# Mixing the weights of the last 1024 tokens one step apart instead of two, in a fused attention and feed-forward kernel

## The chip, the cores and the metric

The kernel runs on one core of one Trainium2 chip. The metric is the device time of one execution in microseconds (us). TensorE is called PE below, VectorE DVE, ScalarE ACT, GpSimd POOL and SyncE SP.

## The reference, cut to what matters

```python
# attention: B, H, S, D = 4, 8, 768, 64; n_global = 8, n_local = 96
scores = scale * q @ k.T + bias            # only a band of 96 keys and 8 global keys is kept
a = softmax(scores)
x = (a @ v)                                # reshaped to 3072 tokens x 512
# feed-forward part, d_model 512, d_ff 1024
a = x @ w1
b = x @ w2
h = a * b @ w3
return h @ w_out
```

The tolerance wants nearly float32 accuracy, so each float32 operand is held as a rounded high part and a low part, and each product is made of three matmuls (high by high, high by low, low by high).

## The kernel before, in words

The tokens come in 12 chunks of 256 (four batches of three). Attention runs in 24 steps of two head pairs, two steps for a chunk. The first four steps (0 to 3) are woven by hand with the loading of the weights. The steps 4 to 23 are the loop at lines 924 to 945, and the change is in this loop.

A step does the following. `visit` puts on PE the score matmuls of step s (L528) and, between them, the products of the probabilities with the values of step s - 2 (L637). `rows` makes the biased scores on DVE (L544) and the exponentials on ACT (L545), eight of each. `take` copies the finished attention output out of PSUM (L58 on ACT, L59 on DVE). `back` brings the transposed probabilities of the step before back from memory. `softmax` scales the rows, half of them on ACT (L561) and half on DVE (L563), after two small DVE instructions (L549, L550). `send` transposes on DVE (L598) and writes the result to memory (L600, on SP's queue); in a step in which a batch begins it also clears part of the tile on POOL (L592).

In between, `slices(k)` lets the feed-forward part of earlier chunks (`FeedForward.run`) go on by k pieces. Most pieces are six matmuls of 128x512 on PE. A product in PSUM tile m (L222 to L224) is emptied by ACT (L230) or multiplied by DVE (L232) and then split in high and low (L58, L59); one in PSUM tile o (L255 to L257) is emptied by ACT (L261). There are two PSUM buffers for m and o together, so the product after the next one needs its buffer emptied.

The last 1024 tokens are not done by `run` but after the loop, by a Strassen scheme (`strassen`), which needs sums and differences of blocks of w1 and w2. These are what `mix`, `round_off` and `keep` make, for one of eight weight groups f at a time:

- `mix(f)` on POOL: two additions that put high and low together (L902, into the tile tq) and four subtractions of blocks (L905, into the tile tl).
- `round_off` : ACT rounds tl to th (L910), and POOL takes th from tl in two instructions (L912), which leaves the low part in tl.
- `keep` on SP's queue: two DMAs of 512 KB write th and tl to the tensor tw in memory (L916, L917).

`strassen` reads tw with the loads of L985. The tiles tq, th and tl have one buffer each, so L905 of the next group waits until L917 has read tl.

The orders on PE, ACT, POOL and SP in the loop are those of the program (`manual_schedule`). An engine's instruction that waits holds everything behind it on that engine. The order on DVE is made by the framework's scheduler.

In the kernel before, the mix of group f is put out at the end of step 7 + 2f, and its rounding and writing in step 8 + 2f, so that the last group is written in step 22.

```python
    SLICES = [()] * 3 + [14, 7, 7, 6, 6, 6] + [10, 10] + [9] * 7 + [8, 8, 7, 7, 7, 9]
```

Of the kernel before, what the change touches and what calls it, by code (L numbers as in the profile page):

```python
# [27 lines left out]
NFC = DF // P  # L28
# [5 lines left out]
SLOT = GLB + P  # L34
KW = WIN + NQ * SLOT
BW = WIN + GLB
MIX = 7
UW = BW + P
QW = KW + T
STEP = 2  # L40
# [399 lines left out]
def banded(ctx, tc, ff, xp, ns, nt, one, nf, oki, ident, qk, vx):  # L440
# [68 lines left out]
    def load_values(c, hp, tag="vr"):  # L509
        b, cb = divmod(c, NCB)  # L510
        nw = 2 * NQ if cb else 2 * NQ - 1
        vr = ld.tile([P, STEP, 2 * NQ, 2 * D], F32, tag=tag, name=f"vr_{c}_{hp}")
        nc.sync.dma_start(out=vr[:, :, :nw], in_=vx[b, cb, hp // STEP, :, :, :nw])
        return [vr[:, i] for i in range(STEP)]
# [16 lines left out]
    def rows(c, hp, ps, sm=None):  # L531

        pr = at.tile([P, NQ, 2, UW], F32, tag="pr", name=f"pr_{c}_{hp}")
        mx = at.tile([P, NQ, 2], F32, tag="mx", bufs=3, name=f"mx_{c}_{hp}")
        if sm is None:
            sm = at.tile([P, NQ, 2], F32, tag="sm", bufs=3, name=f"sm_{c}_{hp}")
        for j in range(NQ):
            first = c % NCB == 0 and j == 0
            w0 = BW if first else 0
            for u in range(2):  # L540
                h = 2 * hp + u
                bias = bias0[:, h, :] if first else biasw[:, h, :]
                m = mx[:, j, u:u + 1]
                nc.vector.tensor_tensor_reduce(out=pr[:, j, u, w0:], in0=ps[u][:, j, w0:UW], in1=bias, scale=-SCALE, scalar=3.0e38, op0=ALU.add, op1=ALU.min, accum_out=m)  # L544
                nc.scalar.activation(pr[:, j, u, w0:], pr[:, j, u, w0:], AF.Exp, bias=m, scale=-1.0, accum_out=sm[:, j, u:u + 1])  # L545
        return pr, sm
# [5 lines left out]
    def softmax(c, hp, pr, sm, scaled, inverted=False):  # L552

        if not inverted:
            invert(sm)
        for j in range(NQ):
            w0 = BW if c % NCB == 0 and j == 0 else 0
            for u in range(2):
                x, r = pr[:, j, u, w0:], sm[:, j, u:u + 1]
                if u == 0 or scaled is nc.scalar:  # L560
                    nc.scalar.activation(x, x, AF.Copy, scale=r)  # L561
                else:
                    nc.vector.tensor_scalar(out=x, in0=x, scalar1=r, scalar2=None, op0=ALU.mult)  # L563
        return pr
# [37 lines left out]
    def back(s):  # L602
        if s not in sent:
            return
        x, d = sent.pop(s)
        for b, m0 in enumerate((1, 0, 3, 2)):
            ms = slice(m0, m0 + 5)
            (nc.sync, nc.scalar)[b // 2].dma_start(out=x[b * BK:(b + 1) * BK].rearrange("r k a u c -> r (k a) (u c)")[:, ms], in_=d[:, :, :, b].rearrange("k a r e -> r (k a) e")[:, ms])
        phs[s] = x
# [37 lines left out]
    def slices(k):  # L647
        while k > 0 and work:
            if next(work[0], "end") == "end":
                work.pop(0)  # L650
            else:
                k -= 1

    def loads(s, keys=True, vals=True):
        if s < n and keys:
            qrs[s] = load(*pairs(s)[0])
        if s < n and vals:
            vrs[s] = load_values(*pairs(s)[0])
# [10 lines left out]
    def take(s, uu, late=False):  # L669
        c, h0 = pairs(s)[0]  # L670
        x2 = xs[c // 2]
        if c >= TAIL:
            x = x2[:, h0:h0 + STEP, c % 2 * T:][:, :, :T]
            for o, y in [(x, uu[:, :, :T])] if not isinstance(uu, list) else [(x[:, i], y[:, :T]) for i, y in enumerate(uu)]:
                nc.scalar.activation(o, y, AF.Copy)
            return
        xc = [x[:, :, c % 2 * T:][:, :, :T] for x in x2]
        hi, lo = (x[:, h0:h0 + STEP] for x in xc)
        if late:
            nc.scalar.activation(hi, uu[:, :, :T], AF.Copy)  # L680
            ff.late.append((lo, uu[:, :, :T], hi))
        else:
            for x in [(hi, lo, uu[:, :, :T])] if not isinstance(uu, list) else [(hi[:, i], lo[:, i], x[:, :T]) for i, x in enumerate(uu)]:
                split(nc, *x)
        if h0 + STEP == NP and c < 2:
            work.append(ff.run(c, *xc, c * T, T))
        elif h0 + STEP == NP and c % 2:
            work.append(ff.run(c, *x2, (c - 1) * T, W))

    def visit(s, sv, ahead):  # L690


        uu = None if sv is None else spread(sv)
        ps = [None, None]

        def some(i):
            ps[i] = scores(*pairs(s)[i], qrs[s][i])

        def half(k):
            if uu is not None:  # L700
                if k:
                    nc.scalar.activation(uu[:, :, T], ident[:, :STEP], AF.Copy)
                values([uu[:, i] for i in range(STEP)], sv, k)

        if ahead:
            some(0)
        half(0)
        if not ahead:
            some(0)
        some(1)  # L710
        half(1)
        return ps, uu
# [31 lines left out]
    def send(s, prs):  # L744
        for i, (pr, sm) in enumerate(prs):
            swap(s, i, pr)
# [150 lines left out]
    def mix(f):  # L897

        th, tl = tg.tile([P, 4, 2 * P], F32R, name="th"), tg.tile([P, 4, 2 * P], F32, name="tl")
        q = tg.tile([P, 2, NCC * P], F32, name="tq")  # L900
        for i in range(2):
            nc.gpsimd.tensor_tensor(out=q[:, i], in0=ff.wq[0][:, f, i].bitcast(F32), in1=ff.wq[1][:, f, i].bitcast(F32), op=ALU.add)  # L902
        (b11, b21), (b12, b22) = ((q[:, i, :2 * P], q[:, i, 2 * P:]) for i in range(2))
        for o, x, y in ((2, b12, b11), (0, b22, tl[:, 2]), (1, b22, b12), (3, b21, tl[:, 0])):
            nc.gpsimd.tensor_tensor(out=tl[:, o], in0=x, in1=y, op=ALU.subtract)  # L905
        mixed.append((f, th, tl))

    def round_off():
        f, th, tl = mixed[-1]
        nc.scalar.activation(th, tl, AF.Copy)  # L910
        for i in range(0, 4, 2):
            nc.gpsimd.tensor_tensor(out=tl[:, i:i + 2], in0=tl[:, i:i + 2], in1=th[:, i:i + 2].bitcast(F32), op=ALU.subtract)  # L912

    def keep():
        f, th, tl = mixed.pop(0)
        nc.sync.dma_start(out=tw[f, :, 0], in_=th.bitcast(F32))  # L916
        nc.sync.dma_start(out=tw[f, :, 1], in_=tl)  # L917

    SLICES = [()] * 3 + [14, 7, 7, 6, 6, 6] + [10, 10] + [9] * 7 + [8, 8, 7, 7, 7, 9]
    with tc.manual_schedule(engines={mybir.EngineType.PE}):  # L920
        with tc.manual_schedule(engines={mybir.EngineType.DVE, mybir.EngineType.SP}):
            first_steps()
        with tc.manual_schedule(engines={mybir.EngineType.Activation, mybir.EngineType.SP, mybir.EngineType.Pool}):
            for s in range(SWAP + 1, n):
                sv = s - 2 if s > SWAP + 1 else None
                ps, uu = visit(s, sv, True)
                rs = []
                for i, p in enumerate(pairs(s)):
                    rs.append(rows(*p, ps[i]))
                    if i == 0 and uu is not None:  # L930
                        take(sv, uu)
                loads(s + 1, vals=False)
                loads(s - 1, keys=False)
                back(s - 1)
                if 0 <= s - MIX < 2 * NFC and (s - MIX) % 2:
                    round_off()
                slices(2)
                for p, r in zip(pairs(s), rs):
                    softmax(*p, *r, nc.vector)
                send(s, rs)  # L940
                if mixed:
                    keep()
                if 0 <= s - MIX < 2 * NFC and (s - MIX) % 2 == 0:
                    mix((s - MIX) // 2)
                slices(SLICES[s] - 2)
            back(n - 1)
            vrs[n - 1] = load_values(*pairs(n - 1)[0], tag="qr")
            x0 = xs[TAIL // 2]
            ah = {k: both(xp, t, k) for k, t in (("a11", "xh"), ("a12", "xl"))}
            for i, y in enumerate(ah.values()):  # L950
                slices(3)
                split(nc, y[:, 0], y[:, 1], x0[:, i * NCC // 2:][:, :NCC // 2])
            slices(SLICES[n - 1] - 6)
            last_visit()
        ctx.close()
        strassen(tc, ff, xp, tw, x0, xs[TAIL // 2 + 1], ah, slices)
        assert not work


def both(pool, tag, name):  # L960
    return pool.tile([P, 2, NCC // 2, W], F32R, tag=tag, name=name)
# [314 lines left out]
```

## Time and profile before

| | |
|---|---|
| time, median of 3 runs (lowest to highest) | 526.68 us (526.28 to 527.04) |
| profiled execution: its own time | 527.25 us |
| its span, first to last instruction | 525.4 us |
| busy PE / DVE / ACT / POOL | 512.7 / 367.0 / 266.7 / 108.7 us |
| mean granted clock of PE | 0.999 of full |

The profiled execution has 1.85 us around its span. The busy time of an engine is an average over stages; what a change is worth is read from the stretch in which it lies, here from step 7 (about 138 us) to step 22 (about 366 us).

### The profile page before, as it was taken

The page shows a single profiled execution, that of the slowest core. Times are in us where ns is not written, and L with a number is a line of the kernel's source. Part 1 is how long each engine was busy: PE and PEld are TensorE (multiplying, and loading weights), DVE is VectorE, ACT ScalarE, POOL GpSimd, SP SyncE. Part 2 cuts the span into 40 slices and gives each one's busy share as a digit, 9 for nine tenths or more (in the row PEclk, how much of TensorE's full clock was granted, in tenths as well). Part 3 has the DMA queues.
Part 4 walks back from the last instruction along what each step waited for, and adds up shares of the span by engine and source line. Part 5 has one row for each costly group of instructions (what it writes and reads, how often), then busy time and mean ns, then how long its engine had stood idle before and what let it go on. Part 6 is the DMA issues. An engine that isn't in the chain of part 4 may idle for free. (4 is left out here: it accounts for less than half of the span.)

```text
span 525.4 us, 11328 instructions
## 1 busy us (share of the span) xinstructions
PE 512.7 (98%) x4234; PEld 407.8 (78%) x4234; DVE 367.0 (70%) x944; ACT 266.7 (51%) x745; POOL 108.7 (21%) x123
## 2 busy tenths in 40 slices
PE   8899999999999999999999999999999999999995
PEld 3445469889988888888888888788888888888884
DVE  8999997976787576665667746688527545556663
ACT  1354776576676554556655554667434332443330
POOL 1000000000225050243205024422000649600001
PEclk9999999999999999999999999999999999999999
DMA  8987845377778766776856597877624327464414
GB/s 318 420 329 252 308 173 176 119 248 255 258 238 291 247 209 208 256 259 200 297 189 236 172 331 249 280 234 292 217 90 136 109 95 261 173 224 130 134 61 168
DMA packets 55827, 116.12 MB, mean 221 GB/s; under 512 B 5010, under 2 KB 32786, under 8 KB 55762
## 3 DMA queue, kind: packets, MB, share of 16 engines
q1 hardware_dynamic: 47698, 106.58, 57.8%
q10 hardware_dynamic: 7680, 7.41, 5.2%
q0 software_dynamic: 384, 1.31, 0.9%
q8 instruction: 35, 0.57, 0.5%
q14 instruction: 30, 0.25, 0.1%
HBM read 73.86 MB, written 40.89 MB: 218 GB/s over the span
## 5 line engine op out<-in xcount | busy, mean ns | idle before, releaser
L222 PE MATMUL m<-xh,wqh 128*128 128x512 f32 (+1 forms) x320 | 113.5, 355 | 1.8 <-DVE ring_a L232 1.2
L223 PE MATMUL m<-xl,wqh 128*128 128x512 f32 (+1 forms) x320 | 111.0, 347 | 0.0
L224 PE MATMUL m<-xh,wql 128*128 128x512 f32 (+1 forms) x320 | 110.9, 347 | 0.0
L545 ACT ACTIVATE pr<-pr,mx 128x232 f32<-128x232 f32 (+1 forms) x192 | 88.2, 461 | 10.4 <-DVE mx L544 10.4
L222 PEld LDWEIGHTS m<-xh,wqh 128*128 128x128 f32 x320 | 60.5, 189 | 11.8 <-DVE ring_a L232 1.6
L544 DVE CUSTOM_DVE_ANT_0 pr<-s,biasw 128x232 f32<-128x232 f32 x160 | 53.9, 395 | 19.3 <-PE s L528 19.2
L224 PEld LDWEIGHTS m<-xh,wql 128*128 128x128 f32 x320 | 60.5, 189 | 7.7
L223 PEld LDWEIGHTS m<-xl,wqh 128*128 128x128 f32 x320 | 60.6, 189 | 7.2
L598 DVE STREAM_TRANSPOSE ph<-pr 128x512 f32<-128x512 f32 x84 | 49.1, 641 | 3.2 <-ACT pr L561 2.1
L255 PE MATMUL o<-wh,gh 128*128 128x512 f32 x128 | 50.7, 396 | 0.0
L257 PE MATMUL o<-wh,gl 128*128 128x512 f32 x128 | 49.9, 390 | 0.0
L256 PE MATMUL o<-wl,gh 128*128 128x512 f32 x128 | 49.9, 390 | 0.0
L912 POOL TENSOR_TENSOR tl<-tl,th 128x512 f32<-128x512 f32 x16 | 21.8, 1384 | 112.0 <-ACT th L910 112.0
L58 ACT ACTIVATE gh<-ring_a 128x512 fp32r<-128x512 f32 x29 | 18.3, 630 | 50.8 <-DVE ring_a L232 47.9
L232 DVE TENSOR_TENSOR ring_a<-m,ring_a 128x512 f32<-128x512 f32 x32 | 21.8, 683 | 26.2 <-PE m L224 24.7
L528 PE MATMUL s<-qr 64*64 64x168 f32 (+2 forms) x768 | 36.5, 299 | 0.0
L991 DVE TENSOR_TENSOR us<-b,us 128x512 f32<-128x512 f32 x17 | 11.7, 690 | 35.3 <-PE b L998 25.2
L545 ACT ACTIVATION_READ_ACCUMULATOR pr<-pr,mx 128x1 f32 x192 | 36.1, 188 | 0.0
L561 ACT ACTIVATE pr<-pr,sm 128x232 f32<-128x232 f32 (+1 forms) x84 | 33.3, 466 | 2.5 <-DVE sm L550 2.5
L637 PE MATMUL v<-ph,vr 64*64 64x64 f32 (+2 forms) x1208 | 34.0, 243 | 0.0
L637 PEld LDWEIGHTS v<-ph,vr 64*64 64x64 f32 (+1 forms) x1208 | 32.1, 133 | 1.3 <-issue 0.4
L199 PE MATMUL w<-wo,ta 128*128 128x512 f32 x64 | 29.4, 602 | 2.3 <-DVE ta L166 1.6
(209 smaller groups left out, 925.5 us busy)
## 6 DMA issues: line engine op xcount, KB each, us to landing
d<-ph SPq DMA_DIRECT2D x42, 512.0 KB, 3.2
t<-tw SPq DMA_DIRECT2D x48, 256.0 KB, 3.1
qr<-qk SPq DMA_DIRECT2D x16, 624.0 KB, 4.3
vr<-vx SPq DMA_DIRECT2D x17, 512.0 KB, 6.5
ph<-d SPq DMA_DIRECT2D x42, 160.0 KB, 6.0
ph<-d ACTq DMA_DIRECT2D x42, 160.0 KB, 5.9
raw<-w3t SPq DMA_DIRECT2D x11, 512.0 KB, 8.8
qr<-qk SPq DMA_DIRECT2D x8, 520.0 KB, 4.6
```

What stands on the lines that cost most here:

```text
L222: nc.tensor.matmul(ps[:, z], lhsT=mh, rhs=xh[:, i], start=i == 0, stop=False)
L223: nc.tensor.matmul(ps[:, z], lhsT=mh, rhs=xl[:, i], start=False, stop=False)
L224: nc.tensor.matmul(ps[:, z], lhsT=ml, rhs=xh[:, i], start=False, stop=i == NCC - 1)
L255: nc.tensor.matmul(ps, lhsT=gh[:, f, ts], rhs=self.wh[:, f], start=f == 0, stop=False)
L256: nc.tensor.matmul(ps, lhsT=gh[:, f, ts], rhs=self.wl[:, f], start=False, stop=False)
L257: nc.tensor.matmul(ps, lhsT=gl[:, f, ts], rhs=self.wh[:, f], start=False, stop=f == NFC - 1)
L528: nc.tensor.matmul(ps[u][g * HQ:(g + 1) * HQ, j, cols], lhsT=m[:, q0:q0 + HQ], rhs=m[:, j * SLOT:][:, cols], start=True, stop=True)
L544: nc.vector.tensor_tensor_reduce(out=pr[:, j, u, w0:], in0=ps[u][:, j, w0:UW], in1=bias, scale=-SCALE, scalar=3.0e38, op0=ALU.add, op1=ALU ...
L545: nc.scalar.activation(pr[:, j, u, w0:], pr[:, j, u, w0:], AF.Exp, bias=m, scale=-1.0, accum_out=sm[:, j, u:u + 1])
L561: nc.scalar.activation(x, x, AF.Copy, scale=r)
L598: nc.vector.transpose(x[:, k, :, u1 - 4 + u0:u1], units[:, u0:, k0:k0 + P].rearrange("p u (b c) -> p b u c", c=BK))
L637: nc.tensor.matmul(uu[i][u * D:(u + 1) * D, j * P + q:j * P + q + n], lhsT=v[r], rhs=x[:, q // step:(q + n) // step][r], start=k == 0 and ...
```

## The change

The constant MIX goes from 7 to 9, and the conditions in the loop change so that a mix stands in every step from 9 to 16, and a rounding and a write in every step from 10 to 17. Before, mixes stood in steps 7, 9, ..., 21 and roundings and writes in steps 8, 10, ..., 22. No instruction is added or removed.

```diff
-MIX = 7
+MIX = 9
...
                 back(s - 1)
-                if 0 <= s - MIX < 2 * NFC and (s - MIX) % 2:
+                if 0 < s - MIX <= NFC:
                     round_off()
                 slices(2)
...
                 if mixed:
                     keep()
-                if 0 <= s - MIX < 2 * NFC and (s - MIX) % 2 == 0:
-                    mix((s - MIX) // 2)
+                if 0 <= s - MIX < NFC:
+                    mix(s - MIX)
                 slices(SLICES[s] - 2)
```

NFC is 8. The tiles and the functions `mix`, `round_off` and `keep` stay as they are.

## Rows read from the trace of the kernel before

**Rows 1.** The page: span, and busy time of PE with share and instructions.
```profile
span 525.4 us, 11328 instructions
PE 512.7 (98%) x4234; PEld 407.8 (78%) x4234; DVE 367.0 (70%) x944; ACT 266.7 (51%) x745; POOL 108.7 (21%) x123
```

**Rows 2.** Waits of PE, 120 to 395 us: line, releaser, us in total, times, longest.
```profile
PE m L222 <- ACT ring_a L230: 0.6, 1, 0.6
PE m L222 <- DVE ring_a L232: 0.5, 1, 0.5
```

**Rows 3.** Timeline, step 20: start, us, engine, instruction, [idle before <-releaser].
```profile
331.62 1.05 ACT L910 ACTIVATE th<-tl 128x1024 fp32r<-128x1024 f32 x1
332.57 0.58 ACT L230 ACTIVATE ring_a<-m 128x512 f32<-128x512 f32 x1
...
333.20 0.50 PE L222 MATMUL m<-xh,wqh 128*128 128x512 f32 x1 [0.56 <-ACT ring_a L230]
```

**Rows 4.** Timeline, step 7, POOL and DVE.
```profile
140.99 2.55 POOL L902 TENSOR_TENSOR tq<-wqh,wql 128x512 f32<-128x512 f32 x2
...
141.19 1.13 DVE L549 TENSOR_SCALAR sm<-sm 128x4 f32<-128x4 f32 x1 [0.33 <-ACT pr L545]
...
142.57 1.31 DVE L563 TENSOR_SCALAR pr<-pr,sm 128x128 f32<-128x128 f32 x2
```

**Rows 5.** L912 and L917 by source line: ns min/median/max, first and last start; landing.
```profile
L912 POOL TENSOR_TENSOR tl<-tl,th x16: 1285/1300/1762, 156.9 to 359.4; 128x512 f32<-128x512 f32 x16
...
L917 SPq DMA_DIRECT2D tw<-tl x8: 664/1090/1207, 161.3 to 363.5; - x8
...
DMA to landing us min/median/max: 4.6/5.5/6.5
```

**Rows 6.** Timeline, SP, POOL and ACT from step 10 into step 11.
```profile
187.92 0.93 SPq L600 DMA_DIRECT2D d<-ph  x2
...
194.46 0.73 POOL L905 TENSOR_TENSOR tl<-tq 128x256 f32<-128x256 f32 x1 [4.95 <-DMA tw<-tl]
...
196.65 0.74 POOL L905 TENSOR_TENSOR tl<-tq,tl 128x256 f32<-128x256 f32 x1
...
198.81 0.48 ACT L545 ACTIVATE pr<-pr,mx 128x232 f32<-128x232 f32 x1
```

**Rows 7.** Timeline, DVE and SP of step 11, ACT and PE of step 12.
```profile
200.29 0.58 DVE L563 TENSOR_SCALAR pr<-pr,sm 128x232 f32<-128x232 f32 x2
201.07 0.69 DVE L59 TENSOR_TENSOR gl<-ring_a,gh 128x512 fp32r<-128x512 f32 x1 [0.20 <-ACT gh L58]
201.83 2.49 DVE L598 STREAM_TRANSPOSE ph<-pr 128x512 f32<-128x512 f32 x4
...
203.75 0.93 SPq L600 DMA_DIRECT2D d<-ph  x2
...
213.98 1.05 ACT L910 ACTIVATE th<-tl 128x1024 fp32r<-128x1024 f32 x1
...
216.79 0.57 ACT L230 ACTIVATE ring_a<-m 128x512 f32<-128x512 f32 x1
...
217.95 0.39 PE L255 MATMUL o<-wh,gh 128*128 128x512 f32 x1
```

**Rows 8.** Timeline, SP of step 15, ACT, DVE and PE of step 16.
```profile
263.69 0.93 SPq L600 DMA_DIRECT2D d<-ph  x2
...
274.17 1.05 ACT L910 ACTIVATE th<-tl 128x1024 fp32r<-128x1024 f32 x1
...
275.77 1.38 DVE L59 TENSOR_TENSOR gl<-ring_a,gh 128x512 fp32r<-128x512 f32 x1 [0.46 <-ACT gh L58]
...
277.16 0.58 ACT L230 ACTIVATE ring_a<-m 128x512 f32<-128x512 f32 x1
...
277.85 0.45 PE L222 MATMUL m<-xh,wqh 128*128 128x512 f32 x1
```

**Rows 9.** Timeline, SP: the first reads of tw after the loop.
```profile
393.94 3.23 SPq L985 DMA_DIRECT2D t<-tw  x5
```

## The prediction

> **What bounds the kernel now.** I read the page first. PE is busy for 512.7 of 525.4 us [rows 1], so time can come only out of PE's gaps, or be lost by making new ones. The waits of PE in the stretch that the change touches come next: there are two in 275 us, 0.6 us for an eviction by ACT (L230) and 0.5 us for a product on DVE (L232) [rows 2]. All other gaps of PE lie outside the stretch. A change that only moves POOL, ACT and DMA work between steps 7 and 22 can therefore give back at most 1.1 us there, 0.2% of the time, and that is also about what a measurement of this kernel can tell from no change. What it can cost is not bounded that way.
>
> Both waits are children of the work that is moved. In step 20, ACT goes from the last exponential straight to the rounding L910, 1.05 us, and only then to the eviction L230. That ends at 333.15, and PE, which needed the buffer 0.56 us earlier, starts at 333.20 [rows 3]. The other wait lies at 146.8 us, in step 7. There POOL's additions L902 start at 140.99, and a DVE instruction on 4 columns that starts at 141.19 takes 1.13 us: it ends at 142.32, when the first of the two additions (half of 2.55 us, to 142.27) is over [rows 4]. DVE comes late by this, and its product L232 too.
>
> **What goes, what comes, what it costs.** No instruction is added or removed: 64 POOL, 8 ACT and 16 DMA instructions change their place.
>
> *Step 20 loses its rounding.* Without 1.05 us in front of it, L230 ends at 332.1, before PE needs the buffer at 332.64 (333.20 less the 0.56 us of waiting) [rows 3]. This gives back 0.56 us. What comes next on ACT, L561, is then earlier too, so nothing takes the stall's place.
>
> *The mix of group 0 does not move.* Its place in the program goes from step 7 to step 9, but between the two POOL's queue has nothing left but that mix: the rounding of step 8 is gone and the next clearing of a tile comes in step 12. It waits for no buffer, since tq and tl are empty, and the weights have long been there. It starts where it does now, at about 141 us, right after POOL's last clearing, and the 0.5 us on PE stays [rows 2, 4]. I cost this at nothing, with a gain of 0.5 us as the other end.
>
> *Step 10 stays as it is; steps 12, 14 and 16 keep their rounding; steps 11, 13, 15 and 17 get one.* In a step that gets one, 1.05 us of ACT comes after the last exponential. In step 11 that would be 199.29 to 200.34 (the last one starts at 198.81 and takes 0.48) [rows 6]. The split L59 in the same step starts at 201.07 after its L58 [rows 7], so ACT has a hole there that the rounding fills almost wholly. Its direct cost on PE I take as nothing; the other end is the 0.56 us that the same insertion costs in step 20 [rows 3].
>
> *POOL's instructions L912, 1.30 us each [rows 5], follow the rounding and now meet DVE in steps 11 and 15.* There L563 and L59 come just then, and the transposes L598 behind them [rows 7]. What a meeting costs is in two rows: the pair L563 takes 1.31 us in step 7 beside POOL and 0.58 us in step 11 without, +0.73 [rows 4, 7]; L59 takes 1.38 us in step 16 beside L912 and 0.69 us in step 11 without, +0.69 [rows 7, 8]. Together the transposes come 1.42 us later. The low end is 0, if DVE's scheduler orders these otherwise. The high end is 2.2 us: two L912 of 1.30 from 200.45, just behind the rounding, to 203.05; half of the pair L563 (0.29) behind the first, L59 (0.69) behind the second, and L598 at 204.03 where it now starts at 201.83 [rows 5, 7].
> The Trainium skill ("SBUF — State Buffer", section "Who interferes with whom") says that such DVE instructions and a GpSimd instruction share a port pair that is locked for a whole instruction, so that the later one blocks fully. The row of L549 agrees; by that rule alone the delay would be the high end of 2.2 us, and the rule speaks against packing POOL's work into fewer steps.
>
> *Each mix now has one step, not two, before its rounding.* This is the disputed part. ACT's L910 of the next step waits for the last L905, L905 waits for the DMA L917 to read tl, and L917 stands behind L600 on SP's queue. The chain is in the trace between steps 10 and 11, because the mix already runs ahead there: L600 at 187.92, first L905 at 194.46, last one over at 197.39, 9.47 us after L600 [rows 6]. The rounding in step 11 would start at 199.29, so it is ready 1.9 us ahead. For the pairs of steps that have no such chain now I add 9.47 to L600:
> - steps 11 to 12: 203.75 + 9.47 = 213.22, with the delay of 1.42 us of the transposes 214.64, against a rounding at 213.98 [rows 7]. ACT waits 0.66 us, and behind it stand L58, L561 and L230. L230 ends at 217.36 now, and PE needs the buffer at 217.95 [rows 7], a margin of 0.59. PE waits 0.07 us.
> - steps 15 to 16: 263.69 + 1.42 + 9.47 = 274.58 against 274.17 [rows 8]. ACT waits 0.41 us. L230 ends at 277.74, PE needs it at 277.85 [rows 8], a margin of 0.11. PE waits 0.30 us.
> - the other pairs I cost at nothing: 10 to 11, 14 to 15 and 16 to 17 have the chain of step 10 now, ready before the last exponential; in 12 to 13 and 13 to 14 the step before gets no meeting of L912 with L563 ahead of the transposes, and PE is in long products into o.
> With a delay of 0 the two sum to 0. With 2.2 us they give 0.85 + 1.08 = 1.93 us.
>
> *SP's queue and the DMAs.* L916 and L917 are moved ahead of the key and value loads of the steps 12, 14, 16 and 18. In step 10 the writes are issued by 190.7 and nothing on SP's queue comes before 195 us, so they pass in a hole. The last write comes at 363.5 now, the first read of tw at 393.94 [rows 5, 9]; being earlier gains nothing.
>
> *Sum.* -0.56 + 0.07 + 0.30 = -0.2 us, with the ends -0.56 and +1.37 us. Against the profiled execution this is 525.4 - 0.2 = 525.2 of span and 527.05 us with the 1.85 us around it. That execution was 0.57 us above the median of the runs, so the forecast is 526.5 us.
>
> **The rivals.**
> *The rounding waits (slower).* The place is ACT's queue in steps 12 and 16, where L905 of the step before isn't done. It decides from the point at which the transposes of steps 11 and 15 come later than 1.35 us (step 12, 213.98 + 0.59 - 213.22) and 0.62 us (step 16, 274.17 + 0.11 - 273.16). For it: step 16 has hardly any margin, and the DMA's landing spreads from 4.6 to 6.5 us around 5.5 [rows 5]. Against it: step 10's chain is ready 1.9 us early, and PE's own waiting gives the chain of the next step nothing more to do. Price: 1.93 us at a delay of 2.2, and 1.0 us more in each of the two steps if the landing takes its longest, 3.93 us. Less 0.56, it gives 528.0 to 530.0 us; its middle is 529.0.
> *All is hidden.* The scheduler of DVE puts L59 behind the transposes, or the chain is quicker: both new waits are nothing and only the 0.56 us remains, 526.1 us. For it: the hole on ACT in step 11. Against it: it needs all steps to go well.
> *Faster.* Group 0's mix moves with its place, away from DVE's busy stretch in step 7, or DVE's new order takes that stall away: another 0.5 us, 525.6 us. Against it: nothing on POOL holds that mix back.
>
> **How the numbers follow.** The forecast has 0.44, "all is hidden" 0.21, the rounding that waits 0.27, faster 0.08. The predicted time is that of the forecast, 526.5. The range goes down to 525.7, just above the case of both stalls gone, and up to 529.0, the middle of the slower rival; what lies above (0.14) and below (0.06) is left out. Faster by over 0.2% (below 525.6) has 0.07, a little less than its case, which ends just there. Slower by over 0.2% (above 527.7) has the 0.27 of its rival, and the rest, 0.66, is the same.
>
> **What would show it.** Right: PE's wait at step 20 is gone and the one of step 7 is there; the first L902 starts at about 141 us; L59 and L563 are longer in steps 11 and 15; POOL's L905 end within half a microsecond of the rounding in steps 12 and 16; the waits of PE from 120 to 395 us sum to 0.8 to 1.0 us. Wrong: ACT's L910 shows idle time put down to POOL of a microsecond or more in several steps, and PE waits for L230 or L261 in each of them; or the transposes of steps 11 and 15 start where they do now; or a new wait of PE comes from DVE, whose order can change with the plan in all steps from 8 to 22.

## The result, and the profile after

The changed kernel takes 529.87 us (median of 5 runs, 529.30 to 531.77) beside 527.04 us for the kernel before on the same chip (5 runs, 526.28 to 527.23): 0.6% more, ratio 1.006 with a 95% interval of 1.0046 to 1.0075. It is slower, where no change was forecast. The profiled execution is the slowest of the five, 531.77 us.

The page of the changed kernel, as in [rows 1], with the granted clock in 40 slices:

```profile
span 530.0 us, 11328 instructions
PE 514.4 (97%) x4234; PEld 409.1 (77%) x4234; DVE 365.3 (69%) x944; ACT 267.0 (50%) x745; POOL 108.9 (21%) x123
...
PEclk9999999999999999999998999999999999999999
```

The span is 4.6 us longer, PE's busy time only 1.7 us, and one slice of the clock has dropped. The waits of PE from 120 to 400 us, as in [rows 2] (line, releaser, us in total, times, longest):

```profile
PE m L222 <- ACT ring_a L230: 2.3, 1, 2.3
PE o L255 <- ACT ring_a L230: 0.8, 1, 0.8
PE m L222 <- DVE ring_a L232: 0.5, 1, 0.5
```

The wait of step 20 is gone (0.56 us), that of step 7 is there as before (0.5 us), and two new ones stand in steps 12 and 16, 0.76 and 2.30 us. Both are waits for the eviction L230 on ACT. The timeline of step 11 shows how the first begins, on SP, DVE and POOL (as in [rows 7]):

```profile
196.17 0.55 SPq L506 DMA_DIRECT2D qr<-qk  x1
...
200.96 1.63 DVE L563 TENSOR_SCALAR pr<-pr,sm 128x232 f32<-128x232 f32 x2
...
201.07 2.66 POOL L912 TENSOR_TENSOR tl<-tl,th 128x512 f32<-128x512 f32 x2 [2.99 <-ACT th L910]
...
202.51 1.78 DVE L59 TENSOR_TENSOR gl<-ring_a,gh 128x512 fp32r<-128x512 f32 x1
204.21 2.48 DVE L598 STREAM_TRANSPOSE ph<-pr 128x512 f32<-128x512 f32 x4
...
206.12 0.93 SPq L600 DMA_DIRECT2D d<-ph  x2
```

The pair L563 takes 1.63 us and not 0.58, L59 takes 1.78 and not 0.69 [rows 7], both beside L912. L600 comes 9.95 us after the key load of its step (L506, at 196.17); before, it was 8.24 us, from this load to 203.75 [rows 7]:

```profile
195.51 0.56 SPq L506 DMA_DIRECT2D qr<-qk  x1
```

The transposes' write is 1.71 us late. Then step 12, on POOL, ACT and PE, in the kernel after:

```profile
213.06 0.82 POOL L905 TENSOR_TENSOR tl<-tq 128x256 f32<-128x256 f32 x1 [6.37 <-DMA tw<-tl]
...
215.35 0.73 POOL L905 TENSOR_TENSOR tl<-tq,tl 128x256 f32<-128x256 f32 x1
...
216.12 1.06 ACT L910 ACTIVATE th<-tl 128x1024 fp32r<-128x1024 f32 x1 [1.38 <-POOL tl L905]
...
218.95 0.57 ACT L230 ACTIVATE ring_a<-m 128x512 f32<-128x512 f32 x1
...
219.57 0.50 PE L255 MATMUL o<-wh,gh 128*128 128x512 f32 x1 [0.76 <-ACT ring_a L230]
```

It is read from the top: the mix starts when the write of the group before has been read out of tl, it ends at 216.08, ACT has stood idle for 1.38 us in front of its rounding, the eviction behind the rounding is late, and PE waits 0.76 us for the buffer. Steps 15 and 16 are the same with larger numbers (SP, POOL, ACT, PE, as in [rows 8]):

```profile
267.12 0.93 SPq L600 DMA_DIRECT2D d<-ph  x2
...
268.79 1.09 SPq L917 DMA_DIRECT2D tw<-tl  x1
...
275.45 0.74 POOL L905 TENSOR_TENSOR tl<-tq 128x256 f32<-128x256 f32 x1 [7.76 <-DMA tw<-tl]
...
277.69 0.76 POOL L905 TENSOR_TENSOR tl<-tq,tl 128x256 f32<-128x256 f32 x1
...
278.49 1.06 ACT L910 ACTIVATE th<-tl 128x1024 fp32r<-128x1024 f32 x1 [2.42 <-POOL tl L905]
...
281.49 0.57 ACT L230 ACTIVATE ring_a<-m 128x512 f32<-128x512 f32 x1
...
282.11 0.56 PE L222 MATMUL m<-xh,wqh 128*128 128x512 f32 x1 [2.30 <-ACT ring_a L230]
```

From L600 to the end of the mix there are 11.33 us (267.12 to 278.45), where step 10 has 9.47 [rows 6]. The write of tl alone, from its issue to the first L905, takes 6.66 us and not 4.86.

After this gap PE ran slower. The busy time of the engines and, third from the right, the granted clock in stretches of one microsecond:

```profile
281.00:282.00 1.00, 0.00 (x0) 0.00 (x0) 1.00 (x3) 1.00 (x3) 1.00 (x1) 1.00 0.00 0
282.00:283.00 1.00, 0.89 (x3) 0.73 (x4) 1.00 (x3) 0.06 (x1) 1.00 (x2) 0.70 0.00 0
283.00:284.00 1.00, 1.00 (x4) 0.81 (x3) 1.00 (x3) 0.00 (x0) 1.00 (x2) 0.50 0.08 16
...
285.00:286.00 1.00, 1.00 (x4) 0.80 (x3) 0.69 (x1) 0.08 (x1) 0.05 (x1) 0.59 0.79 324
286.00:287.00 1.00, 1.00 (x6) 0.80 (x5) 0.00 (x0) 0.19 (x1) 0.00 (x0) 1.00 1.01 410
```

From 282 to 286 the clock is at 0.70, 0.50, 0.50 and 0.59 of full (284 to 285, left out, is the second 0.50): it fell to 1.2 GHz and went back to 2.4 GHz. That is 0.30 + 0.50 + 0.50 + 0.41 = 1.71 us of PE at full clock. So this execution lost 0.76 + 2.30 + 1.71 and gained 0.56: +4.2 us, where the two spans differ by 4.6. It was also 0.67 us late before anything that the change moves (the clearing L592 that starts at 129.17 before starts at 129.84). The two together are 0.3 us too many; where these were gained wasn't followed up. The other four timed executions, 529.30 to 529.91 us, lie 2.3 to 2.9 us above the kernel before, near the 2.5 us of the waits alone.

### The profile page after: what moved, and what is told of

Same layout as the page of the kernel before. It is cut to its first block, busy times and chain, and to the rows that moved or that the text cites. A ratio compares the mean times of both kernels' runs of the same rounds, so it can differ in the third digit from the quotient of the medians.

```text
span 530.0 us, 11328 instructions
## 1 busy us (share of the span) xinstructions
PE 514.4 (97%) x4234; PEld 409.1 (77%) x4234; DVE 365.3 (69%) x944; ACT 267.0 (50%) x745; POOL 108.9 (21%) x123
## 4 chain that ended last, share of the span: by engine, by line
PE 72%; DVE 15%; DMA 6%; ACT 3%; issue 3%; POOL 1%; SPq 0%; ACTq 0%; DVEq 0%; POOLq 0%
PE a L998 8%; PE m L222 8%; PE m L223 8%; PE m L224 8%; PE o L255 6%; PE o L256 6%; PE o L257 5%; PE s L528 4%; PE v L637 4%; PE oa L1018 4%; PE b L998 4%; DMA tw<-tl 2%; PE c L998 2%; DVE t3s L166 2%; DVE wo L166 2%
## 5 line engine op out<-in xcount | busy, mean ns | idle before, releaser
L545 ACT ACTIVATE pr<-pr,mx 128x232 f32<-128x232 f32 (+1 forms) x192 | 88.2, 461 | 10.5 <-DVE mx L544 10.5
L58 ACT ACTIVATE gh<-ring_a 128x512 fp32r<-128x512 f32 x29 | 18.2, 629 | 50.6 <-DVE ring_a L232 50.5
L545 ACT ACTIVATION_READ_ACCUMULATOR pr<-pr,mx 128x1 f32 x192 | 36.1, 188 | 0.0
L59 DVE TENSOR_TENSOR gl<-ring_a,gh 128x512 fp32r<-128x512 f32 x29 | 25.3, 872 | 13.3 <-ACT gh L58 13.3
L912 POOL TENSOR_TENSOR tl<-tl,th 128x512 f32<-128x512 f32 x16 | 21.5, 1362 | 53.6 <-ACT th L910 53.6
```

## The experiments

Theory: each rounding waits, at the head of ACT's queue, for a mix that waits for the write of the group before, and what ACT holds back is the eviction that PE needs. Rivals: DVE and POOL meeting on their port explains it alone; the new places of the roundings explain it; the packed schedule is worse in itself. Diffs are against the changed kernel unless another is named.

**e8, the changed kernel once more**, for a second profile.

> The changed kernel once more, for a second profile of it. The first one had granted clock 0.74 of full from 280 to 285 us, after PE's gap of 2.30 us, and was 1.9 us longer than the median of its five timed runs, 529.87 us. Theory (the clock falls in some executions and not in others, and the median is the waits of PE alone, 0.76 + 2.30 - 0.56 = 2.5 us above the kernel before): PE's two gaps are there again within 0.3 us; without a stretch below full clock the profiled execution is at 529 to 530 us, with one at 531 to 532 us. Rival (the fall belongs to the gap): it is there again, and all times lie at 531 us or more.

The median is 531.61 us of 6 runs beside 527.02 (ratio 1.0077, 1.0056 to 1.0097). Five of the runs lie at 531.39 to 532.25 with a mean clock of 0.994 or 0.995, one at 528.38 with 1.000. In the profiled one (531.39 us) PE's gaps are 0.80 and 2.30 us, ACT's waits 1.38 and 2.42 us, and the clock goes down to half again:

```profile
282.00:283.00 1.00, 1.00 (x3) 0.73 (x3) 1.00 (x3) 0.00 (x0) 1.00 (x2) 0.50 0.08 16
...
284.00:285.00 1.00, 1.00 (x4) 0.82 (x3) 0.32 (x1) 0.63 (x1) 0.62 (x1) 0.50 0.95 377
```

Neither expectation holds whole. The gaps repeat to 0.04 us. The fall came in both profiles. That it needn't come is argued and not shown: of the eleven timed executions of this kernel, the six from 531.39 us up have a mean clock of 0.994 or 0.995 and the five up to 529.91 us have 0.998 to 1.000, but none of the five was profiled. On this reading the two medians, 529.87 and 531.61 us, mix executions of two kinds.

**e5, one buffer in place.** The differences are made in the tile of the sums itself, so the additions too wait for the write: the same chain, 2.55 us longer.

```diff
-        q = tg.tile([P, 2, NCC * P], F32, name="tq")
+        q = tl.rearrange("p (i k) c -> p i (k c)", i=2)
...
-        for o, x, y in ((2, b12, b11), (0, b22, tl[:, 2]), (1, b22, b12), (3, b21, tl[:, 0])):
-            nc.gpsimd.tensor_tensor(out=tl[:, o], in0=x, in1=y, op=ALU.subtract)
+        for o, x, y in ((b11, b12, b11), (b12, b22, b12), (b22, b22, b11), (b21, b21, b22)):
+            nc.gpsimd.tensor_tensor(out=o, in0=x, in1=y, op=ALU.subtract)
```

The loads in `strassen` take the blocks in the new order.

> The kernel of the two buffers in place with one buffer again: now the two additions too have to wait for the write of the group before, so the chain from the write to the end of the mix is 2.55 us longer than in the changed kernel. Theory (ACT's wait for this chain is the cost): ACT waits about 0.7 us in step 11, 3.9 in step 12, 5 in step 16 and 1 to 3 us in the others of 11 to 17, PE waits 8 to 14 us in all, and the clock falls behind the long ones; 536 to 546 us. Rival (making the differences in place is what helped, not the second buffer): 525 to 527 us.

540.79 us beside 527.15 (ratio 1.0256, 1.0228 to 1.0285). The waits of PE from 120 to 400 us, and ACT's wait for the mix from 100 to 400 us:

```profile
PE m L222 <- ACT ring_a L230: 5.0, 2, 4.3
PE m L222 <- ACT ring_o L261: 2.8, 1, 2.8
PE o L255 <- ACT ring_a L230: 2.4, 1, 2.4
...
ACT th L910 <- POOL tl L905: 15.2, 5, 4.4
```

A chain 2.55 us longer makes ACT wait in five steps (0.95, 3.92, 2.55, 3.39 and 4.42 us in 11, 12, 13, 14 and 16), PE waits over 10 us, and the clock falls twice, at the gaps of 2.84 and 4.30 us, but not at one of 2.44 us.

**e1, two buffers in place**: e5 with one word more. It needs no more room than the changed kernel, since tq is gone.

```diff
-        th, tl = tg.tile([P, 4, 2 * P], F32R, name="th"), tg.tile([P, 4, 2 * P], F32, name="tl")
+        th, tl = tg.tile([P, 4, 2 * P], F32R, name="th"), tg.tile([P, 4, 2 * P], F32, name="tl", bufs=2)
```

> The changed kernel, with the four subtractions made in place in the tile of the sums and that tile held in two buffers, so that no mix waits for the write of the group before. Theory (ACT waits for a mix that waits for the DMA that reads tl): ACT's rounding never waits for POOL, PE's waits in steps 12 and 16 (0.76 and 2.30 us in the profile of the changed kernel) are gone, the clock stays up, and only the 0.5 us of step 7 remains: 526.1 to 526.7 us. Rival (port contention and late transposes alone): the transposes of steps 11 and 15 are still 1.7 us late and the time stays at 529 us or more.

525.46 us (11 runs) beside 526.85 (27 runs), ratio 0.9981, 0.9972 to 0.9990: it beats both kernels. PE has no wait between 100 and 400 us. POOL's waits show why, since none is for a DMA any more:

```profile
POOL tl L912 <- ACT th L910: 79.7, 8, 36.9
POOL ph L592 <- PE v L637: 69.6, 4, 38.1
```

L600 of steps 11 and 15 is as late as in the changed kernel here (9.93 and 9.94 us after the key load). So late transposes alone cost nothing, and neither does a rounding in each step: the cost is the wait for the write. The wait of step 7 is gone too, 0.5 us that aren't the schedule's (see e6).

**e3, the writes of th and tl ahead of those of the transposes** on SP's queue.

```diff
-                send(s, rs)
                 if mixed:
                     keep()
+                send(s, rs)
```

> The changed kernel with the writes of th and tl put on SP's queue ahead of the writes of the transposes in the same step, not behind them. Theory (the chain from L600 over L917 to L905 is too long by 1.4 and 2.4 us in steps 12 and 16): L917 is issued about 3 us earlier, right behind L912, the mix is ready before ACT's slot in all steps, PE waits 0.5 us only, 526.1 to 526.7 us. Rival (L600 is now late behind L917 and the transposed rows come back late): PE waits at the values matmuls L637 and the time is above that of the kernel before.

526.15 us beside 526.85 (ratio 0.9986, 0.9977 to 0.9995). With the write issued at 263.87 in step 15, the mix is over at 270.25 and not at 278.45:

```profile
266.87 0.74 POOL L905 TENSOR_TENSOR tl<-tq 128x256 f32<-128x256 f32 x1
...
269.53 0.72 POOL L905 TENSOR_TENSOR tl<-tq,tl 128x256 f32<-128x256 f32 x1
```

ACT does not wait, and PE's only wait is that of step 7 (0.48 us). L600 of steps 11 and 15 isn't later for it (9.95 us after the key load in both), because L912 is done before the transposes are.

**e9, the rounding behind the scaling of the rows** in ACT's order.

```diff
-                if 0 < s - MIX <= NFC:
-                    round_off()
                 slices(2)
                 for p, r in zip(pairs(s), rs):
                     softmax(*p, *r, nc.vector)
+                if 0 < s - MIX <= NFC:
+                    round_off()
                 send(s, rs)
```

> The changed kernel with the rounding put behind the scaling of the rows in ACT's order, not ahead of the evictions right after the exponentials; all waits for the DMA stay. Theory (the price is set by what stands behind the waiting rounding): the rounding starts 1.5 to 2.3 us later in each step, when the mix of the step before is ready or nearly so; ACT waits less than 0.6 us, PE waits up to 0.5 us in step 16, 0.5 us in step 7, nothing else above 0.2; 526.0 to 527.2 us. Rival (what holds PE is the late mix, wherever the rounding stands): the mix of the next step is later by as much, ACT waits as long as before and PE still 2 us or more in step 16; 529 us or more.

527.28 us beside 527.02 (ratio 1.0008, 1.0000 to 1.0017). Every wait for a DMA stays in the program, but the rounding meets a finished mix and ACT does not wait for POOL; the waits of PE:

```profile
PE m L222 <- ACT ring_a L230: 0.5, 1, 0.5
PE m L222 <- DVE ring_a L232: 0.5, 1, 0.5
PE o L255 <- ACT ring_a L230: 0.2, 1, 0.2
```

The 0.5 and 0.2 us are the rounding's own 1.05 us ahead of L230 in steps 16 and 12. But the edit changes more than the place in ACT's queue, because L912 moves with the rounding. It no longer meets L563 and L59, and L600 of steps 11 and 15 is on time (8.25 and 8.31 us after the key load). From step 15 into 16, on SP, ACT and POOL:

```profile
263.92 0.93 SPq L600 DMA_DIRECT2D d<-ph  x2
...
273.95 0.48 ACT L545 ACTIVATE pr<-pr,mx 128x232 f32<-128x232 f32 x1
...
274.47 0.74 POOL L905 TENSOR_TENSOR tl<-tq,tl 128x256 f32<-128x256 f32 x1
...
277.20 1.04 ACT L910 ACTIVATE th<-tl 128x1024 fp32r<-128x1024 f32 x1
```

The mix is over 0.78 us behind the last exponential (275.21 and 274.43), where the changed kernel has 2.48 us (278.45 and 275.97). Most of the gain is thus put down to the transposes being on time. What the place in the queue is worth for an equally late mix isn't shown: e7 below has transposes on time and the rounding in its old place, and there PE waits 0.57 us in step 16, nearly the 0.50 us of e9.

**e4, odd steps, two apart.** The kernel before with one number changed.

```diff
-MIX = 7
+MIX = 8
```

> The kernel before with MIX at 8: mixes in steps 8, 10, ..., 22, roundings in 9, 11, ..., 23, still two steps apart. The roundings fall into the steps that did not have one, and L912 meets DVE in steps 11 and 15, but every mix has two steps. Theory (the spacing is the cost, not the new places): transposes of steps 11 and 15 are 1.7 us late as in the changed kernel, ACT never waits for POOL, PE has no wait above 0.6 us; 526.1 to 527.3 us. Rival (the odd steps themselves do not bear the rounding): PE waits of 0.7 us or more in steps 12 and 16 or in the odd steps, 528 us or more.

527.13 us beside 526.85 (ratio 1.0012, 1.0003 to 1.0021). L912 meets DVE in steps 11 and 15, and L600 there comes 9.94 us after the key load, as late as in the changed kernel, but no rounding waits. PE's waits, 100 to 400 us:

```profile
PE m L222 <- DVE ring_a L232: 0.9, 2, 0.5
```

They are 0.47 us in step 7 and 0.44 us in step 12, where DVE is late. The new places cost nearly nothing; it is the spacing that costs.

**e7, no sums.** The mix takes the high parts of w1 and w2 alone, and the two subtractions after the rounding are left out, so the last 1024 tokens lack low parts.

```diff
-        for i in range(2):
-            nc.gpsimd.tensor_tensor(out=q[:, i], in0=ff.wq[0][:, f, i].bitcast(F32), in1=ff.wq[1][:, f, i].bitcast(F32), op=ALU.add)
+        q = ff.wq[0][:, f].bitcast(F32)
...
-        for i in range(0, 4, 2):
-            nc.gpsimd.tensor_tensor(out=tl[:, i:i + 2], in0=tl[:, i:i + 2], in1=th[:, i:i + 2].bitcast(F32), op=ALU.subtract)
```

> The changed kernel without the two additions (the mix takes the high parts alone) and without the two subtractions after the rounding, so the output of the last 1024 tokens lacks low parts. POOL does nothing between ACT's rounding and the landing of the write, so DVE meets it only in the four differences. Theory (late transposes start the chain): the transposes of steps 11 and 15 are on time, L600 is about 8.2 us behind the key load of its step as in the kernel before and not 9.9, the mix ends 9.5 to 10 us later, ACT waits less than 0.3 us, PE less than 1 us in all; 525.8 to 527 us. Rival (the write in every step is slow by itself): ACT still waits 0.7 us or more in step 16, 527.5 us or more.

526.48 us beside 527.15 (ratio 0.9987, 0.9978 to 0.9996). L600 is on time (8.24 and 8.30 us after the key load in steps 11 and 15). In step 12 the mix is ready 0.68 us ahead. Step 16 still waits; SP, POOL, ACT and PE there (the same instructions have other line numbers, L903 for L905, L908 for L910):

```profile
263.01 0.93 SPq L600 DMA_DIRECT2D d<-ph  x2
...
271.31 0.74 POOL L903 TENSOR_TENSOR tl<-wqh 128x256 f32<-128x256 f32 x1 [14.04 <-ACT pr L545]
...
274.33 1.06 ACT L908 ACTIVATE th<-tl 128x1024 fp32r<-128x1024 f32 x1 [0.73 <-POOL tl L903]
...
277.96 0.50 PE L222 MATMUL m<-xh,wqh 128*128 128x512 f32 x1 [0.57 <-ACT ring_a L230]
```

The profile names an exponential (L545) as what ended POOL's wait, the last event before it; I take it to be the write, which was issued 6.62 us earlier, as in the changed kernel (6.66). This parts the 2.30 us of step 16 in two: 0.57 us are there with transposes on time, from a chain that is 11.28 us long (263.01 to 274.29); the other 1.73 us are put down to the late transposes (1.63 us: L600 of step 15 is 9.94 us after the key load in the changed kernel and 8.31 before). It also holds for the rival that it names, with 0.73 us of waiting on ACT, but not for its time.

**e2, no subtraction after the rounding** (the low parts stay unreduced). Meant to take the meeting with DVE away, it didn't: the additions of the next mix move up into the place of L912.

```diff
-        for i in range(0, 4, 2):
-            nc.gpsimd.tensor_tensor(out=tl[:, i:i + 2], in0=tl[:, i:i + 2], in1=th[:, i:i + 2].bitcast(F32), op=ALU.subtract)
```

> The changed kernel without POOL's two subtractions of th (L912), so the low parts of the mixed weights are left unreduced and the output of the last 1024 tokens is not that of the reference. It takes away the meeting of L912 with DVE in steps 11 and 15 but keeps every wait for a DMA. Theory that the late transposes start the chain: L600 of steps 11 and 15 is 1.7 us earlier, the mix is ready 9.5 to 10 us after it, which is before ACT's slot in steps 12 and 16, PE waits 0.5 us only, 526.1 to 526.7 us. Rival (the writes are slow because they now come in each step, whatever the transposes do): the mix of step 15 still comes 11.3 us after L600, ACT waits about 0.7 us in step 16 and PE 0.6 us there; 526.8 to 527.6 us.

529.64 us beside 526.85 (ratio 1.0047, 1.0033 to 1.0061). L600 in steps 11 and 15 comes 9.60 and 10.19 us after the key load, so the transposes are as late as ever. ACT waits in three steps, and DVE is late once more (waits of ACT for POOL, of PE; the second line holds step 7 too):

```profile
PE m L222 <- ACT ring_a L230: 1.6, 1, 1.6
PE m L222 <- DVE ring_a L232: 1.1, 2, 0.7
...
ACT th L910 <- POOL tl L905: 3.0, 3, 1.7
```

It is inconclusive for its question; e7 is the run for it.

**e6, the kernel before with two buffers in place**: the edit of e1 with mixes in steps 7, 9, ..., 21.

> The kernel before (a mix in every second step from 7) with the differences in place in two buffers. There no rounding waits for a mix, so the second buffer has nothing to free. Theory: the wait of 0.56 us in step 20 stays, since the rounding still stands ahead of the eviction; the time is that of the kernel before within 0.2%, 526.0 to 527.2 us, and so what the two buffers give over the kernel before in the packed schedule is the schedule's own. Rival: the gain of the two buffers in place has nothing to do with the schedule, 525.4 us here too.

527.36 us beside 527.15 (ratio 0.9998, 0.9987 to 1.0009). PE's waits, 100 to 400 us:

```profile
PE v L637 <- DVE mx L544: 1.2, 1, 1.2
PE m L222 <- ACT ring_a L230: 0.6, 1, 0.6
```

The 0.56 us of step 20 stays, as the theory has it. The wait of step 7 is gone here as in e1 and e5, so that belongs to the differences in place. The 1.2 us is a new wait at 139.7 us, just ahead of step 7's old one; why it is there wasn't followed up. Without the packed schedule the two buffers gain nothing, this new wait included.

## Why the prediction was wrong

- *Step 20 gives back 0.56 us.* Right: that wait is gone from the profile after, and stays in e6, where the rounding stays.
- *The mix of group 0 does not move, and the wait of step 7 stays.* Right: 0.5 us there, and the first addition again follows right behind POOL's clearing.
- *POOL meets DVE in steps 11 and 15, and the transposes come 1.42 us late, between 0 and 2.2.* Right in kind, too small in size: 1.71 and 1.63 us. In step 11 the pair L563 lost 1.05 and L59 1.09 us, where the rows had 0.73 and 0.69; the 0.20 us that L59 waited for L58 before [rows 7] took up a part. By the port rule of the Trainium skill ("SBUF — State Buffer", "Who interferes with whom") the later of the two engines is blocked for the whole instruction, from which the prediction's estimate was 2.2 us; the loss of the two instructions, 2.14 us, agrees with it.
- *Each mix ends 9.47 us after L600.* This is the step that failed. It was read from the one pair of steps that showed it, 10 to 11, and carried over to all. It was 9.96 us from step 11 and 11.33 us from step 15, and 9.5 to 10.5 us from the other five, so the one row that the forecast took is the shortest; e7 has 11.28 from step 15 with transposes on time, so it isn't the delay that lengthens it. With measured terms the prediction's own sum gives: step 12, 203.75 + 1.71 + 9.96 - 213.98 = 1.44 us of waiting on ACT (1.38 measured), less the margin of 0.59 is 0.85 on PE (0.76); step 16, 263.69 + 1.63 + 11.33 - 274.17 = 2.48 (2.42), less 0.11 is 2.37 (2.30). The mechanism and the margins were right, and no rounding waited in the other pairs, as forecast; the forecast of 0.37 us for the two is 3.06 us, of which 1.86 is the chain in step 16. The spread of the landing, 4.6 to 6.5 us [rows 5], was used for the rival's price and not for the forecast.
- *The rival: the rounding waits.* This is what happened, in its place (ACT in steps 12 and 16) and within its price of 528.0 to 530.0 us. It had a chance of 0.27; the known margin of 0.11 us in step 16 spoke for more. The delay from which PE is held in step 16 is given as 0.62 us, but 274.17 + 0.11 - 273.16 is 1.12; the forecast's 0.30 us there was worked out without this slip.
- *No term for the clock.* A gap of 2.3 us was outside what the sum foresaw, so its second cost, 1.7 us in both profiled executions, was nowhere. It lifts the median of e8 out of the rival's price too.
- *The rule speaks against packing.* Not so here: with the write issued earlier (e3) the packed schedule is 0.1% faster than the kernel before, though L563 and L59 still meet POOL. With the wait for the write taken away (e1) it is 0.2% faster, but there about 0.5 of the 1.4 us is step 7's wait, which the packing doesn't touch.

## What to carry to other kernels

When work is moved closer together, look for the buffer that the old spacing hid: the time from the last use to the reuse (here write, landing, four instructions) has to fit in the new spacing with its longest landing, and not with the one that happens to be in the trace. Price it at the head of the queue in which the waiting instruction stands, by what stands behind it: here an eviction with 0.11 us to spare, so that 2.42 us of ACT's waiting became 2.30 us of PE's. Before giving up a tighter schedule, try a second buffer; computing in place may make the room for it.

## What the runs showed of the hardware

PE's clock fell to half at gaps of 2.30 us (twice), 2.84 and 4.30 us (e5), but not at one of 2.44 us (e5) or 1.57 us (e2); at the longest it was down before PE went on (0.50 of full from 288 us, PE goes on at 290.00). Matmuls of 128x512 then follow each other every 0.43 us and not every 0.23. The wait of 2.30 us so cost 4.0 us, 1.7 times its length.

From the issue of the write of tl to the first L905 it takes 6.6 us in step 15 in the changed kernel, e4 and e7 alike (6.0 in e9, where L917 is issued later behind the transposes), and 4.9 us in steps 10 and 14. In e7 its last two microseconds, 268.9 to 271.0 us, move little:

```profile
DMA packets 44, 0.13 MB, mean 61 GB/s; under 512 B 17, under 2 KB 17, under 8 KB 43
```

61 GB/s is against 410 GB/s from 266 to 268 us. From 269 to 270 us the 16 DMA engines are busy for 0.06 of the time, about one sixteenth, as if one of them had been left behind with its share. Whether it is so, and what holds it back, stays open.
